# A delta-rule attention and a feed-forward block on one core: the first triangular solve done in two passes by rows

## The chip, the cores and the metric

The kernel runs on one core of a Trainium2 chip. A core has a matrix engine (TensorE, PE in the profile), a vector engine (VectorE, DVE), a scalar engine (ScalarE, ACT), a general engine (GpSimd, POOL) and an engine that here issues the loads and stores (SyncE, SP). Each runs its own list of instructions in order and waits on semaphores. The metric is the device time of one execution in microseconds (us), less being better.

## The reference

The input is q, k, v (4 batches, 8 heads, 768 steps, 48 wide) and beta. A state of 48 by 48 for each batch and head goes through the steps one by one; the answers of all heads are then the tokens (3072 by 384) of a feed-forward block.

```python
k_n = k / (np.linalg.norm(k, axis=-1, keepdims=True) + 1e-06)
for t in range(S):
    kt, vt, bt = (k_n[:, :, t], v[:, :, t], beta[:, :, t, None])
    y[:, :, t] = np.einsum('bhd,bhde->bhe', q[:, :, t], state)
    v_old = np.einsum('bhde,bhd->bhe', state, kt)
    state = state + bt[:, :, :, None] * np.einsum('bhd,bhe->bhde', kt, vt - v_old)
...
x = np.ascontiguousarray(attn_out.transpose(0, 2, 1, 3)).reshape(B * S, H * D)
...
h = x @ w_in          # 384 x 2048
g = h - np.tanh(h)
return (g @ w_out).astype(np.float32)
```

## The kernel before

The 768 steps are cut into 24 chunks of 32. Inside a chunk the recurrence is a linear system: the matrix of inner products of the chunk's keys (the gram, L123), below its diagonal and weighted with beta, plus the identity, has to be inverted for each of the 4 batches and 8 heads. Four chunks make a group (six groups), and one group's 4 x 8 x 4 = 128 systems lie on the 128 partitions of VectorE, which solves them together, column by column: `times` (L246) forms the product of a column with a row, `plus` (L253) adds it to what is left. A group has 30 such columns, and in groups 1 to 5 the middle 21 of them are cut by `spans` into two pieces, so that the second piece of an instruction stands between two that depend on each other.

Group 0 goes another way, since all the rest waits for it. Its four grams are masked and gathered by VectorE (`gather`, L148), turned once (L184), and the 32 x 32 systems are split in halves of 16 (`halves`), which needs 14 columns of 2 x 16 x 16 and then, for each chunk, a join on TensorE of the two halves: `join_a` (L311), a scaled copy on ScalarE (`join_y`, L314), `join_b` (L323), and a last addition on VectorE (`join_u`, L328). Three transposes of half size (L270, L275, L276) lie between.

With the inverse a chunk goes through `chunk` (C, the product with the values, L351), `spread` (sd, L399, a copy on ScalarE or VectorE), `update_product` (U, the state, L361), `answer` (A, L367), `keep` (kp, L402) and the turning of the answer into token columns (`xh`, `xl`). The next chunk begins with `keyed` (K) and `vsub` (vs), which subtracts the state's product, and then its own `chunk`.

Four chunks are a window of 512 tokens of the feed-forward block. There each of 16 blocks of the hidden layer is a product `hidden` (h, L479), `tanh` on ScalarE (th, L487), `gate` on VectorE (ga, L492: h minus tanh h), the split of the result in a high and a low part (gh, L497; gl, L502), and a product `output` (o, L514). Window 0 is done in two halves of 256 columns, so it has 32 gates, the first half with the answers of chunks 0 and 1. All products of the block are in 32-bit parts of that kind, and so the weights too are split on arrival: `sign` (dr, L436) and `low_bits` (db, L442) on ScalarE, `merge` (dm, L447) on VectorE, `high` (dh, L453) on ScalarE, `low` (dl, L457) on VectorE.

The order of every instruction on every engine is written out by hand in one long string, ORDER. An item is engine, operation and arguments: `V:sv:0:40` is step 40 of the solve of group 0 on VectorE, `P:fi:5:-1` is five products of no use (`fill`, L556, 128 x 512 in bf16) on TensorE, `S3:lw:10:1` is the load of weight 10 on SyncE, which may begin when the load three ahead of it has landed (S3: three in flight). The numbers at an item's end are buffers.

## Time and profile before

| | |
|---|---|
| median of three runs | 594.56 us (591.32, 594.56, 595.45) |
| profiled execution: its span | 588.6 us |
| median less the span | 6.0 us (what lies around the span) |
| TensorE busy in the span | 558.4 us, 95% |
| VectorE busy | 379.7 us, 65% |
| ScalarE busy | 187.5 us, 32% |
| GpSimd busy | 39.0 us, 7% |
| read and written in main memory | 42.44 MB and 4.72 MB |

The profile is that of one execution. Its times count from the first instruction, and the 6.0 us are the start and the end around it. Busy shares are means over the whole; the start, up to the first hidden block, and the rest have different limits.

### The profile page before, as it was taken

How to read it: one execution, taken by the hardware profiler on the slowest of the kernel's cores; microseconds unless marked ns; L12 is line 12 of the kernel's file. 1: busy time of each engine (PE TensorE's matmuls, PEld its weight loads, DVE VectorE, ACT ScalarE, POOL GpSimd, SP SyncE). 2: the span in 40 equal slices, each digit the busy share in tenths (PEclk: the TensorE clock that was granted, in tenths of full speed). 3: DMA queues.
4: the chain of work that ended last, by engine and by line, in shares of the span. 5: the costliest groups of instructions: out<-in, count | busy, mean ns of one | idle time of the engine just before them, and what ended most of it. 6: DMA issues, size and time to landing. Idle time of an engine off the chain costs nothing.

```text
span 588.6 us, 25934 instructions
## 1 busy us (share of the span) xinstructions
PE 558.4 (95%) x11943; PEld 458.4 (78%) x11943; DVE 379.7 (65%) x1089; ACT 187.5 (32%) x330; POOL 39.0 (7%) x44
## 2 busy tenths in 40 slices
PE   4848899999999999999999999999999999999997
PEld 3444788899998888788888788787888888888885
DVE  4899997899768995569965333599824322533242
ACT  1447776333313222232222223132320323322211
POOL 0000001100100000000000000200010000001111
PEclk9967999999999999999999999999999999999999
DMA  7778753331325100433312103221210100000001
GB/s 203 236 235 288 220 157 106 107 96 52 105 94 158 47 14 11 144 86 106 91 48 83 30 1 111 70 63 60 62 29 33 52 2 3 1 33 22 2 0 53
DMA packets 21517, 48.82 MB, mean 83 GB/s; under 512 B 3232, under 2 KB 9760, under 8 KB 21408
## 3 DMA queue, kind: packets, MB, share of 16 engines
q1 hardware_dynamic: 20864, 46.44, 26.0%
q8 instruction: 93, 1.52, 1.1%
q10 hardware_dynamic: 544, 0.72, 0.4%
q14 instruction: 16, 0.13, 0.1%
HBM read 42.44 MB, written 4.72 MB: 80 GB/s over the span
## 4 chain that ended last, share of the span: by engine, by line
PE 87%; DVE 9%; issue 2%; DMA 1%; ACT 1%
PE po L514 35%; PE ph L479 34%; PE sums L361 3%; PE g L123 3%; PE pu L351 3%; PE kk L340 3%; PE py L367 2%; PE py L355 2%; DVE ta L246 2%; DVE a L253 2%; PE px L412 1%; DVE raw L447 1%; DMA k<-in_kp 1%; DVE w L457 1%; DMA raw<-in_w_in 1%
## 5 line engine op out<-in xcount | busy, mean ns | idle before, releaser
L514 PE MATMUL po<-gh,w 128*128 128x512 f32 (+1 forms) x1008 | 221.6, 366 | 0.0
L479 PE MATMUL ph<-xt,w 128*128 128x512 f32 (+1 forms) x1008 | 218.4, 364 | 0.5 <-DVE t L492 0.4
L479 PEld LDWEIGHTS ph<-xt,w 128*128 128x128 f32 x1008 | 170.1, 189 | 31.6 <-DVE t L492 0.5
L514 PEld LDWEIGHTS po<-gh,w 128*128 128x128 f32 x1008 | 168.5, 189 | 30.3 <-DVE gh L502 0.2
L492 DVE TENSOR_TENSOR t<-ph,t 128x512 f32<-128x512 f32 (+1 forms) x112 | 68.2, 611 | 108.6 <-ACT t L487 108.4
L487 ACT ACTIVATE t<-ph 128x512 f32<-128x512 f32 (+1 forms) x112 | 59.7, 538 | 192.7 <-PE ph L479 144.7
L502 DVE TENSOR_TENSOR gh<-t,gh 128x512 fp32r<-128x512 f32 (+1 forms) x89 | 54.4, 614 | 26.0 <-ACT gh L497 25.3
L497 ACT CAST gh<-t 128x512 fp32r<-128x512 f32 (+1 forms) x63 | 35.8, 570 | 83.1 <-PE po L514 52.9
L253 DVE TENSOR_TENSOR a<-a,ta 128x108 f32<-128x108 f32 (+28 forms) x269 | 60.4, 257 | 1.5
L246 DVE TENSOR_TENSOR ta<-a 128x108 f32<-128x108 f32 (+28 forms) x269 | 59.6, 254 | 1.3
L502 POOL TENSOR_TENSOR gh<-t,gh 128x512 fp32r<-128x512 f32 (+1 forms) x23 | 27.4, 1193 | 416.9 <-DVE gh L497 215.0
L351 PEld LDWEIGHTS pu<-v,tt 32*32 32x32 f32 x1536 | 27.8, 106 | 9.5 <-issue 4.1
L351 PE MATMUL pu<-v,tt 32*32 32x48 f32 x1536 | 31.6, 212 | 2.4 <-issue 1.4
L340 PEld LDWEIGHTS kk<-st,k 48*32 48x32 f32 x1472 | 27.8, 105 | 6.8 <-issue 3.8
L367 PE MATMUL py<-ub,pc 32*32 32x48 f32 x1536 | 30.9, 209 | 0.4 <-ACT ub L399 0.3
L355 PE MATMUL py<-st,k 48*32 48x48 f32 x1472 | 31.1, 212 | 0.0
L340 PE MATMUL kk<-st,k 48*32 48x48 f32 x1472 | 30.9, 211 | 0.0
L497 DVE CAST gh<-t 128x512 fp32r<-128x512 f32 (+1 forms) x49 | 18.4, 376 | 18.2 <-PE po L514 17.8
L367 PEld LDWEIGHTS py<-ub,pc 32*32 32x32 f32 x1536 | 26.7, 103 | 1.4 <-ACT ub L399 0.6
L355 PEld LDWEIGHTS py<-st,k 48*32 48x32 f32 x1472 | 27.2, 105 | 0.4 <-DVE t L492 0.4
L361 PEld LDWEIGHTS sums<-ub,kt 32*48 32x48 f32 x1472 | 18.9, 119 | 8.4 <-issue 4.7
L361 PE MATMUL sums<-ub,kt 32*48 32x48 f32 x1472 | 21.9, 205 | 1.8 <-ACT ub L399 1.0
(87 smaller groups left out, 386.7 us busy)
## 6 DMA issues: line engine op xcount, KB each, us to landing
c<-in_kp SPq DMA_DIRECT2D x20, 448.0 KB, 4.6
k<-in_kp SPq DMA_DIRECT2D x20, 448.0 KB, 4.0
raw<-in_w_in SPq DMA_DIRECT2D x16, 384.0 KB, 4.1
raw<-in_w_out SPq DMA_DIRECT2D x16, 384.0 KB, 4.2
v<-in_vn SPq DMA_DIRECT2D x24, 192.0 KB, 2.6
kt<-in_kn SPq DMA_DIRECT2D x24, 192.0 KB, 2.9
out<-o SPq DMA_DIRECT2D x17, 256.0 KB, 3.0
k<-in_kp SPq DMA_DIRECT2D x6, 224.0 KB, 4.5
```

Of the source, the lines that this page charges most:

```text
L246: V.tensor_tensor(tv[..., x], P(slice(j + 1, size), slice(j, j + 1)).broadcast_to(d), P(slice(j, j + 1), x).broadcast_to(d), ALU.mult)
L253: V.tensor_tensor(rest, rest, tv[..., x], ALU.add)
L340: nc.tensor.matmul(hv(live[f"kk{s}"])[q:q + 32, h, :], live[f"k{s}"][rows, 0, 2 * h + b // 2, :], states[s % 2][rows, b // 2, h], start=(h ...
L351: nc.tensor.matmul(hv(live[f"pu{s}"])[rows, h, :], tt[rows, 8 * r + h, :], live[f"v{s}"][rows, h, :], start=True, stop=True)
L355: nc.tensor.matmul(hv(live[f"py{s}"])[q:q + 32, h, :], live[f"k{s}"][rows, 1, 2 * h + b // 2, :], states[s % 2][rows, b // 2, h], start=(h ...
L361: nc.tensor.matmul(sums[HALF[b % 2], b // 2, h * D:h * D + D], live[f"kt{s}"][rows, h, :], live[f"ub{s}"][rows, h], start=(s == 0 and h == ...
L367: nc.tensor.matmul(hv(live[f"py{s}"])[to:to + 32, h, :], live[f"pc{s}"][rows, h, :], live[f"ub{s}"][rows, h, :], start=(s == 0 and h == 0) ...
L479: nc.tensor.matmul(p, wi[:, a, c, :], xt[:, b, c, part], start=(i == 0), stop=(i == len(steps_) - 1))
L487: nc.scalar.activation(t, live[name("ph", w, f, z)][:, :n], AF.Tanh)
L492: nc.vector.tensor_tensor(t, live[name("ph", w, f, z)][:, :n], t, ALU.subtract)
L502: (nc.vector if eng == "V" else nc.gpsimd).tensor_tensor(gh[:, 1, :n], live[name("t", w, f, z)][:, :n], gh[:, 0, :n].bitcast(F32), ALU.sub ...
L514: nc.tensor.matmul(live[f"po{NC * w + c}"][:, part], wo[:, a, 128 * c:128 * c + 128], gh[:, b, :n], start=(f == 0 and (a, b) == SPLIT[0] a ...
```

## The change

Group 0 is solved in two passes, chunks 0 and 1 and then 2 and 3 (`rows(0)`, `rows(1)`). Of each pass the two chunks' grams go to one PSUM bank (`grams`), and one transpose reads them from there, without mask or gather, and writes each system twice, into two lanes of 16 partitions for each batch: one lane keeps the even rows of the inverse, the other the odd ones. The inverse starts as the identity (`identity`, on GpSimd) and is built from column 31 down to 1, with `times` (now a scalar_tensor_tensor, whose scalar is read from `gm`, one for each partition) and `plus`, 31 of each in a pass. A transpose of half size (`out_`) hands out each pass's inverse. The joins are gone. The two passes share VectorE: in ORDER their items are interleaved, from step 76 on is the second pass.

Groups 1 to 5 no longer cut their middle columns in two: 60 instructions a group instead of 102, with the same elements. Group 0's beta comes with the constants. All fills use zeros, where they used a block of constants (`wave`) from the second one on. Loads are paced with up to four in flight. The early part of ORDER, up to the first hidden block of window 1 (`P:h:1:0`), is another one; behind it only buffer numbers and the engine of a few items differ (some from GpSimd to VectorE, some from VectorE to ScalarE). In the new order there are 53 fills ahead of chunk 0's `P:C:0`, 11 between it and the first hidden block, and none behind; before there were 29, 31 and 3.

```diff
-    cs = sb.tile([128, 272], F32, name="cs")
+    cs = sb.tile([128, 228], F32, name="cs")
...
-    def gram(s, slot):
-        ps = hc(bank(slot, f"g{s}"))
-        for u in range(16):
-            products(s, ps[:, :, :C], live[f"k{s}"], 0, u)
+    grams = lambda x: sums.rearrange("p r (h c) -> p (r h) c", h=H)[:, :, C * x:C * x + C]
+
+    def gram(s):
+        for r in range(2):
+            for u in range(16):
+                products(s + r, grams(s // 2)[:, H * r:H * r + H], live[f"k{s + r}"], 0, u)
 
     def late(s, slot):
...
     def solve(g, k, *slots):
         if g not in solves:
-            solves[g] = steps(g)
+            solves[g] = steps(g) if g else rows(0) + rows(1)
         solves[g][k](*slots)
 
...
+    def identity():
+        nc.gpsimd.memset(tn, 0.0)
+        for x in range(2):
+            for r in range(2):
+                nc.gpsimd.tensor_copy(tn[:, x].rearrange("p k c -> p (k c)")[:, r::C + 2],
+                                      cs[:, 224 + r:225 + r].broadcast_to([128, C // 2]))
+
+    def rows(x):
+        ss, zz, sq = (small[n] for n in ("ss", "zz", "sq"))
+        nm, gm = small["nm"], half["gn" if x else "gm"]
+        rate, scratch = cs[:, 160 + C * x:160 + C * x + C], (ta, tb)[x]
         V = nc.vector
-        ax = lambda: live[f"a{g}"]
-        sq3 = lambda: ax()[:, :C * C].rearrange("p (i c) -> p i c", c=C)
-        flat = lambda: ax()[:, :C * C]
+        full = lambda: live[f"as{x}"][:, :C * C]
+        a = lambda: full().rearrange("p (i c) -> p i c", c=C)
+        t = tn[:, x]
 
         def turn(slot):
-            make("sol", slot, f"a{g}", [128, 1056])
-            V.transpose(flat(), gs[:, :C * C])
-
-        do = [turn, lambda: V.tensor_copy(sq, flat()[:, ::C + 1])]
-        do.append(lambda: V.tensor_scalar(ss, sq, 1e-30, None, ALU.max))
-        if g == 0:
...
                 lambda: V.tensor_scalar(nm, nm, 0.5, None, ALU.mult)]
         else:
-            do.append(lambda: V.tensor_scalar(nm.bitcast(I32), ss.bitcast(I32), -0.5, 1597463007.0, ALU.mult, ALU.add))
-            for _ in range(3):
-                do += [
-                    lambda: V.scalar_tensor_tensor(zz, ss, -0.5, nm, ALU.mult, ALU.mult),
-                    lambda: V.tensor_tensor(zz, zz, nm, ALU.mult),
-                    lambda: V.scalar_tensor_tensor(nm, zz, 1.5, nm, ALU.add, ALU.mult)]
+            do += newton(nm, ss, zz, sq, gm) + [lambda: V.scalar_tensor_tensor(gm, gm, -1.0, rate, ALU.mult, ALU.mult)]
+        do.append(lambda: V.transpose(turned[x], nm))
+
+        def times(j):
+            k, n = j // 2, C // 2 - j // 2
+            to = scratch[:, j % 2 * 136:j % 2 * 136 + n * j].rearrange("p (k c) -> p k c", c=j)
+            V.scalar_tensor_tensor(to, t[:, k:, j:j + 1].broadcast_to([128, n, j]), gm[:, j:j + 1],
+                                   a()[:, j:j + 1, :j].broadcast_to([128, n, j]), ALU.mult, ALU.mult)
+
+        def plus(j):
+            k, n = j // 2, C // 2 - j // 2
+            V.tensor_tensor(t[:, k:, :j], t[:, k:, :j], scratch[:, j % 2 * 136:j % 2 * 136 + n * j].rearrange("p (k c) -> p k c", c=j), ALU.add)
+
+        for j in range(C - 1, 0, -1):
+            do += [lambda j=j: times(j), lambda j=j: plus(j)]
+        do.append(lambda: V.scalar_tensor_tensor(t, t, -1.0, gm[:, None, :].broadcast_to([128, C // 2, C]), ALU.mult, ALU.mult))
+
+        def out_(slot=None):
+            if x == 0:
+                make("sol", slot, "tt0", [128, 1024])
+            to = live["tt0"][:, :32 * C].rearrange("p (u k z) -> p k z u", k=C // 2, z=2)[:, :, :, 16 * x:16 * x + 16]
+            V.transpose(to, t.rearrange("p k (z u) -> p k z u", z=2))
+
+        do.append(out_)
+        return do
...
-        def spans(j):
-            if nb == 2 or not 5 < j < 27:
-                return (slice(0, j),)
-            x = 4 if j < 14 else 10
-            return (slice(0, x), slice(x, j))
+            n = C - 1 - j
+            return ta[:, j % 2 * 240:j % 2 * 240 + n * j].rearrange("p (i c) -> p i c", c=j), [128, n, j]
 
         def times(j):
             tv, dims = scratch(j)
-            for x in spans(j):
-                d = dims[:-1] + [x.stop - x.start]
-                V.tensor_tensor(tv[..., x], P(slice(j + 1, size), slice(j, j + 1)).broadcast_to(d),
-                                P(slice(j, j + 1), x).broadcast_to(d), ALU.mult)
+            V.tensor_tensor(tv, sq3()[:, j + 1:, j:j + 1].broadcast_to(dims), sq3()[:, j:j + 1, :j].broadcast_to(dims), ALU.mult)
 
         def plus(j):
             tv, _ = scratch(j)
-            for x in spans(j):
-                rest = P(slice(j + 1, size), x)
-                V.tensor_tensor(rest, rest, tv[..., x], ALU.add)
-
-        for j in range(1, size - 1):
...
-    def join_u(s):
-        gs, tn, tt, x = parts(s)
-        upper = tt[:, x:x + 8, C // 2:]
-        nc.vector.scalar_tensor_tensor(upper, jh(live[f"jb{s}"]), half_, upper, ALU.mult, ALU.add)
-
...
     def prep(s, eng):
         g, r = divmod(s, 4)
         v = live[f"v{s}"]
+        nt = live[f"nt{g}"] if g else turned[r // 2]
         (nc.vector if eng == "V" else nc.gpsimd).tensor_tensor(
-            v, v, live[f"nt{g}"][:, 8 * r:8 * r + 8, None].broadcast_to([128, H, D]), ALU.mult)
+            v, v, nt[:, 8 * (r if g else r % 2):, None][:, :8].broadcast_to([128, H, D]), ALU.mult)
 
     def key_product(s, h, b):
...
-                fill_ = wave if fills[0] else wz
-                fills[0] += 1
-                nc.tensor.matmul(ps.rearrange("p (a b) -> p a b", a=4), fill_, wide(fill_, 4), start=True, stop=True)
+                nc.tensor.matmul(ps.rearrange("p (a b) -> p a b", a=4), wz, wide(wz, 4), start=True, stop=True)
...
-V:open A:ka:3:0 S3:lk:2:1 S3:lk:0:2 A:const A:ka:1:3 P:gm:3:0 P:gm:2:1 S2:lb:0:0 P:gm:0:2 S2:lc:4:0 V:gr:0:V:0
...
+V:open A:ka:0:0 A:const G:ti S1:lk:1:1 P:fi:5:-1 P:fi:5:-1 S2:lw:4:0 S3:lk:2:2 S3:lk:3:3 S4:lw:2:1 S4:lq:2:0 S4:lc:5:0
```

On VectorE, in the middle of the first solve, the list before was this (`a` is the matrix being solved, `ta` scratch; L447 and L457 are weights):

```order
L253 TENSOR_TENSOR a_229<-a_229,ta 128x2x4x11
L246 TENSOR_TENSOR ta<-a_229 128x72
L457 TENSOR_TENSOR w_433<-raw_231,w_433 128x2x384
L253 TENSOR_TENSOR a_229<-a_229,ta 128x2x3x12
L246 TENSOR_TENSOR ta<-a_229 128x52
L253 TENSOR_TENSOR a_229<-a_229,ta 128x2x2x13
L246 TENSOR_TENSOR ta<-a_229 128x28
L253 TENSOR_TENSOR a_229<-a_229,ta 128x2x14
```

and now it is this (`ta`, `tb` scratch of the first and second pass, `tn` the inverse being built, `as` the turned grams):

```order
L215 SCALAR_TENSOR_TENSOR ta<-tn,gmh,as_324 128x126
L215 SCALAR_TENSOR_TENSOR tb<-tn,gnh,as_342 128x56
L220 TENSOR_TENSOR tn<-tn,ta 128x9x14
L220 TENSOR_TENSOR tn<-tn,tb 128x2x28
L215 SCALAR_TENSOR_TENSOR ta<-tn,gmh,as_324 128x130
L215 SCALAR_TENSOR_TENSOR tb<-tn,gnh,as_342 128x81
L220 TENSOR_TENSOR tn<-tn,ta 128x10x13
L220 TENSOR_TENSOR tn<-tn,tb 128x3x27
```

Where each step stood next to the one that it depends on, or to a piece of the weights, the steps of the two passes now stand in turn, and the second pass lags behind.

On ScalarE, ahead of the spread of chunk 0 (the copy `ub` of L399, now L365), the list before was this (`pc` and `yj` are copies out of PSUM, `w` and `raw` weights):

```order
L314 ACTIVATE yj_913<-ja_812 128x128
L453 CAST w_954<-raw_523 128x2x384
L314 ACTIVATE yj_961<-ja_674 128x128
L436 ACTIVATE raw_541<-raw_541 128x768
L453 CAST w_968<-raw_427 128x2x384
L442 ACTIVATE raw_541<-raw_541,cs 128x768
L399 COPY ub_981<-pu_915 128x384
L436 ACTIVATE raw_851<-raw_851 128x768
```

and now it is this (`ta` of 128x1 is the load of the tanh table):

```order
L155 COPY pc_600<-l_499 128x256
L408 ACTIVATE raw_108<-raw_108,cs 128x768
L295 ACT_TABLE_LOAD
L295 ACTIVATE ta<-ta 128x1
L402 ACTIVATE raw_401<-raw_401 128x768
L419 CAST w_672<-raw_122 128x2x384
L408 ACTIVATE raw_401<-raw_401,cs 128x768
L365 COPY ub_840<-pu_785 128x384
```

The spread stands behind one load of the table and fewer copies of weights, and the copies for the joins are gone; what is directly ahead of it is `low_bits` of weights 0 and 1, as before.

## Rows read from the trace of the kernel before

**Rows 1.** The span in 40 slices, busy tenths of TensorE and VectorE.

```profile
PE   4848899999999999999999999999999999999997
...
DVE  4899997899768995569965333599824322533242
```

**Rows 2.** Long windows: busy us (instructions) by engine, clock, DMA share, GB/s.

```profile
11.10:47.10 36.00, 22.85 (x925) 15.36 (x926) 31.89 (x103) 15.81 (x26) 3.01 (x7) 0.83 0.79 242
47.10:66.30 19.20, 16.63 (x548) 10.06 (x549) 19.20 (x63) 15.50 (x24) 0.00 (x0) 0.87 0.87 270
66.30:168.40 102.10, 98.76 (x2865) 93.08 (x2863) 89.85 (x279) 46.44 (x90) 7.35 (x8) 1.00 0.38 112
66.30:178.20 111.90, 108.29 (x3288) 101.53 (x3286) 94.38 (x289) 48.31 (x93) 8.08 (x9) 1.00 0.36 107
178.20:588.60 410.40, 406.54 (x6928) 327.79 (x6928) 231.39 (x632) 106.36 (x187) 27.66 (x24) 1.00 0.17 51
```

**Rows 3.** Timeline of VectorE at the start of the solve: start us, us.

```profile
7.82 1.47 DVE L148 TENSOR_TENSOR gs<-g,cs 128x256 f32<-128x256 f32 x3 [5.97 <-PE g L123]
...
11.17 1.25 DVE L184 STREAM_TRANSPOSE a<-gs 128x1024 f32<-128x1024 f32 x1
```

**Rows 4.** Timeline of TensorE: grams, chunk 0, first hidden blocks of windows 0 and 1.

```profile
5.07 2.72 PE L123 MATMUL g<-k 48*32 48x32 f32 x192 [5.07 <-DMA k<-in_kp]
...
47.10 1.49 PE L351 MATMUL pu<-v,tt 32*32 32x48 f32 x61 [0.49 <-ACT pc L155]
...
66.36 2.51 PE L479 MATMUL ph<-xt,w 128*128 128x256 f32 x18
...
178.10 6.56 PE L479 MATMUL ph<-xt,w 128*128 128x512 f32 x27
```

**Rows 5.** Timeline of VectorE: the 32nd gate, the last of window 0.

```profile
168.35 0.42 DVE L492 TENSOR_TENSOR t<-ph,t 128x256 f32<-128x256 f32 x1 [0.41 <-ACT t L487]
```

**Rows 6.** Timeline of VectorE: solve steps, a dependent pair and two neighbours.

```profile
21.95 0.28 DVE L246 TENSOR_TENSOR ta<-a 128x112 f32<-128x112 f32 x1
22.26 0.28 DVE L253 TENSOR_TENSOR a<-a,ta 128x112 f32<-128x112 f32 x1
...
44.91 0.40 DVE L246 TENSOR_TENSOR ta<-a 128x96 f32<-128x96 f32 x2
45.23 0.55 DVE L335 TENSOR_TENSOR v<-v,nt 128x384 f32<-128x384 f32 x1
```

**Rows 7.** VectorE groups by shape, whole span: busy us, mean ns of one.

```profile
L447 DVE SCALAR_TENSOR_TENSOR raw<-raw 128x768 int32<-128x768 int32 x16 | 15.2, 952 | 0.0
...
L502 DVE TENSOR_TENSOR gh<-t,gh 128x256 fp32r<-128x256 f32 x27 | 11.9, 441 | 0.9 <-ACT gh L497 0.6
...
L280 DVE STREAM_TRANSPOSE tt<-a 128x1024 f32<-128x1024 f32 x5 | 10.4, 2074 | 0.0
...
L184 DVE STREAM_TRANSPOSE a<-gs 128x1024 f32<-128x1024 f32 x6 | 7.4, 1232 | 0.2
...
L497 DVE CAST gh<-t 128x256 fp32r<-128x256 f32 x17 | 4.9, 285 | 2.2 <-PE po L514 2.1
...
L246 DVE TENSOR_TENSOR ta<-a 128x170 f32<-128x170 f32 x5 | 1.7, 333 | 0.1
...
L328 DVE SCALAR_TENSOR_TENSOR tt<-jb,cs,tt 128x128 f32<-128x128 f32 x4 | 1.4, 346 | 0.0
```

**Rows 8.** Timeline of ScalarE: the spread of chunk 0.

```profile
52.62 0.47 ACT L399 COPY ub<-pu 128x384 f32<-128x384 f32 x1
```

**Rows 9.** Window of the loads up to the weights that chunk 0 meets.

```profile
0.00:46.00 46.00, 26.29 (x1153) 18.54 (x1157) 33.62 (x102) 16.87 (x26) 3.21 (x11) 0.88 0.77 227
```

**Rows 10.** Windows of 2 us around the clock's fall and rise.

```profile
44.00:46.00 2.00, 1.43 (x38) 0.61 (x42) 1.97 (x11) 0.57 (x1) 0.00 (x0) 0.50 0.85 280
...
52.00:54.00 2.00, 1.05 (x65) 0.81 (x64) 2.00 (x5) 1.93 (x3) 0.00 (x0) 1.00 0.90 287
```

**Rows 11.** Timeline of TensorE: the fills before the rise.

```profile
49.10 3.09 PE L556 MATMUL po<-cs 128*128 128x512 bf16 x7
```

More of the change, by code (lines that the diff above doesn't have):

```diff
@@ L798 @@
     bt = by_parity(beta.reshape(B, H, NS, C).transpose(2, 0, 1, 3).copy())
[L799 to L800 removed]
+    lanes = lambda a: a.reshape(-1, 4, B, H, C).transpose(0, 2, 1, 3, 4).reshape(-1, 128, C)
+    first = lanes(bt[[0, 1, 0, 1, 2, 3, 2, 3]])
+    bt = lanes(bt)
+    const = np.zeros((128, 228), np.float32)
     p, i = np.arange(128)[:, None], np.arange(C)
```

496 lines of the change are left out of this document (229 added, 267 removed).

## The prediction

> **What bounds the kernel now.** The busy shares of the page mislead here: TensorE is at 95% and VectorE at 65% over the whole span, but the slices show two stages [rows 1]. In the first four or five slices VectorE is at 8 or 9 tenths and TensorE often below; after that TensorE stands at 9 to the end and VectorE falls. So I cut the span at the events that matter and read the windows [rows 2]. From the turn of the first solve (11.17, [rows 3]) to chunk 0 (47.10, [rows 4]) VectorE is busy 31.89 of 36.00 us, and from there to the first hidden block (66.36, [rows 4]) all of 19.20. The start is VectorE's. From 66.3 to the last gate of window 0 (168.35, [rows 5]) both are nearly full: TensorE 98.76 of 102.10, VectorE 89.85. From the first hidden block of window 1 (178.10, [rows 4]) on it is TensorE alone, 406.54 of 410.40 [rows 2], and there the change leaves the work as it was. So the question is at what time window 1 begins; what is saved or lost before 178.10 goes one for one into the end.
>
> The account of VectorE to that point: 168.35 - 11.17 = 157.2 us, in which it is idle 4.1, 0 and 12.25 us (the three windows of [rows 2]), so 16.4 idle and 140.8 busy. Window 1 begins 9.75 us behind the 32nd gate [rows 4, 5].
>
> **The work that VectorE gets.** What one step costs must be read from start to start, because an instruction's end overlaps the next one's start. A dependent step of 112 elements starts 0.31 us ahead of the next [rows 6]. The slope from 170 elements (333 ns) to 768 (952 ns) is 619/598 = 1.04 ns an element [rows 7]; the dependent step's fixed part is then 0.31 - 0.116 = 0.19 us. Two neighbours that don't wait for each other, of 168 elements together, take 0.32 us [rows 6], so 0.07 each and the slope. I take 0.07 as the price of a step that has another lane's step behind it.
>
> - Elements of the solves. Group 0 had 28 instructions with 2,240 elements; now it has 4 x 31 = 124 (31 `times` and 31 `plus` in each of two passes) with 4 x 2,856 = 11,424, the sum of (16 - j/2 rounded down) times j over j from 1 to 31. Of groups 1 and 2, whose solves lie ahead of the 32nd gate, 204 instructions become 120, with the same 19,840 elements. So 9,184 elements more: 9,184 x 1.04 = +9.6 us.
> - Their fixed part. The count goes from 232 to 244: +0.8 us if all hide. In group 0's new order 115 of the 124 steps have a neighbour that doesn't need them, as the order of VectorE shows; in groups 1 and 2 each of 120 steps now waits for the one before unless something stands between, and there the order puts gates, weights and gathers between most. I take +1.0, with the upper bound that every one of 115 pays 0.12 more (0.19 - 0.07), +13.8, as a rival of its own below.
> - The scalar from a pointer in 62 `times`. The nearest row is the old join, the same operation with a pointer, 128 elements in 346 ns [rows 7], against 0.29 by slope for 128 elements without one (333 - 42 x 1.04). That is 0.05 at most, since it also reads PSUM; at least 0. I take 0.03: +1.9 (0 to 3.1).
> - Transposes. Away go one of 1.23 [rows 7] and three of half size at some 1.04 (half of 2.07, [rows 7]): 4.35. In come two turns and two of half size. A turn of 1,024 elements reads PSUM with a stride; a contiguous one takes 1.23, one with a strided output 2.07 [rows 7]. I take 1.85, nearer the second, as every element hops: 3.7 + 2.1 = 5.8, so +1.4 (0.1 to 1.9). The Trainium skill, "Vector Engine (DVE) Microarchitecture Reference", section 5.2, "Measured stream behaviour on trn2", has 1.73 ns a column for one source that hops at each element, against 1.054; that is for SBUF and for no transpose, and it would make a turn 1.8 us, an estimate; no run here has shown it yet.
> - Work that changes hands. To VectorE come four `low` parts of a gate at some 0.34 and three scalings of values at some 0.47 (their rows, 441 ns [rows 7] and 0.55 [rows 6], less the overlap of about 0.1): +2.8. From it go five casts (285 ns, [rows 7]), two gathers, and four copies to ScalarE, estimated together at -4.2; the joins' four additions, at about 0.2 each, and a scaling, -1.0.
>
> Sum: 9.6 + 1.0 + 1.9 + 1.4 + 2.8 - 4.2 - 1.0 = **+11.5**, so 152.3 us busy where 140.8 were. With the bounds above, about +8 to +14.
>
> **What VectorE no longer waits for.** The masked gathers begin at 7.82, the turn at 11.17 [rows 3]. The three grams that start when the keys land take 2.72 us from 5.07 [rows 4], 0.9 each. The new turn needs two: 5.07 + 1.8 = 6.9, and I say 7.0. That is 4.2 us of start. With no wait at all the 32nd gate would stand at 7.0 + 152.3 = 159.3. Before, the waits were 16.4 in the same stretch, 4.1 early and 12.25 while TensorE was almost full. They don't all go, since TensorE's own work stands between: gates need hidden blocks, `vsub` needs the state.
>
> Early waits, from the new order of VectorE and ScalarE: merging of weight 4 behind its load, the first turn of group 1 behind the pair of grams that stands behind 14 fills, a merge and a `low` behind ScalarE's chain, POOL's triangle; an estimate of 4.5 us together, like the 4.1 before. Chunk 0: its spread on ScalarE started at 52.62 [rows 8], behind splits of weights. In the new order the splits of weights 0 and 1 are still ahead of it. By the order 10.5 MB are loaded up to weight 1, which at 227 GB/s [rows 9] is 46 us, and with the splits behind it 48 to 49; so the spread comes some 3.5 us earlier, and the first hidden block with it at about 63.5 (61.5 to 66.4). Four in flight rather than three I cost at nothing: the share of the DMA engines is already 0.77 to 0.87 there [rows 2, 9].
>
> From there TensorE has, by [rows 2], 108.29 us of work to 178.10, less three small products and fills that now stand ahead or are gone, an estimate of 3.5: 104.8. If it idled as little as before (3.3 of 102.10, [rows 2]) window 1 would begin at 63.5 + 104.8 + 3.3 = 171.6, seven earlier than before. But VectorE cannot follow: its 32nd gate, with the 4.5 early and some 4.6 of waits later, stands at 159.3 + 9.1 = 168.4, window 1 at 168.4 + 9.75 = 178.15. That is the time of before. The late waits of 4.6 are the weakest number; 12.25 was seen with less work to do. When VectorE is the later of the two its waits shrink, and I take a little over a third.
>
> So span 588.6 + 0.05, and the time is **594.6** by the profiled execution (588.6 + 6.0); the median of the runs shown is 594.56, the same. I write 595.
>
> **Rivals.**
>
> *VectorE keeps up.* Its added work is at the lower bounds (+8) and the late waits fall to 1: 7.0 + 148.8 + 5.5 = 161.3, window 1 by VectorE at 171.1 and by TensorE at 171.6. Seven earlier: 588. For it: 12.25 us of idle time stand in VectorE's window. Against: they came where TensorE was at 97%, so each waits for something that won't come sooner unless the start does. 586 to 589.
>
> *The clock.* The granted clock was 0.50 in the window from 44 to 46 and 1.00 from 52 on [rows 10]; between stand seven fills [rows 11] and what follows. Half of full speed is the lower of its two levels, 1.2 of 2.4 GHz. In the new order 11 fills stand between chunk 0 and the first hidden block where 31 stood, and they are zeros throughout. If the clock is still at half when the hidden blocks begin, a stretch of 10 to 20 us of products at half speed loses 5 to 10, on the engine that has no slack afterwards: 600 to 605. It decides from the granted clock of the 2 us stretches from the first hidden block: at 0.5 this holds, at 1.0 it doesn't. For it: where the clock was at half TensorE was busy 1.43 of 2 us [rows 10], and the stretch from chunk 0 on has 20 fills less now. Against: 53 fills ahead of chunk 0, and the first hidden blocks are dense themselves.
>
> *The lanes don't hide each other.* If a step of one pass costs the dependent price although the other's stands between, the start gets +13.8 us, of which the early waits take back about 4: window 1 at 188, 604. For it: a lane's steps are written as chains. Against: the neighbours of [rows 6] took 0.16 us each for 84 elements on the mean, where a dependent step of that size would take 0.19 + 0.09 = 0.28. The Trainium skill says in "VectorE: DVE Perf Modes", section "The DRAIN you can't avoid", that the next operation does not start until the pipe is empty, and advises fewer operations; by that rule alone this rival holds, and the two neighbours of this trace, started 0.16 us apart, speak against it.
>
> *It doesn't do what it says:* the weights' loads hold chunk 0 where it was (first hidden block at 66). VectorE is then late anyway, and it costs 0 to 2 us: inside the forecast.
>
> **How the numbers follow.** A measurement of this kernel can tell about 1% from no change, 5.9 us: faster is below 588.6, slower above 600.5. The forecast, 591 to 599, has 0.58; VectorE keeping up 0.20 (half to two thirds of it below 588.6, and some of it below 586); the clock 0.13; the lanes 0.09. To leave out no more than 2 in 10 the range goes from 585 to 604. Faster 0.18: most of the first rival and the forecast's lower tail. Slower 0.22: the two others. Same 0.60.
>
> **What would show it.** In the profile after: the first turn at 7.0 and of 1.85 us; steps of L215 and L220 that start 0.07 us plus 1.04 ns an element apart; the spread of chunk 0 at 49, the first hidden block at 63.5, the 32nd gate at 168.4, window 1 at 178.2; VectorE idle 9 us up to that gate, and TensorE idle some 7 from 63.5 on, waiting for gates. I would be wrong if VectorE were idle as before in the stretch with the gates: then its work was never what set that pace, and the earlier start is a gain, or if the granted clock is 0.5 past 62.

## The result and the profile after

The changed kernel took 596.86 us (median of 20 runs, 594.74 to 601.77) where the kernel before took 593.95 (20 runs, 589.45 to 598.03): 1.0063 of its time, 95% interval 1.0039 to 1.0087. It was measured again beside the experiments, on two chips: 1.0136 (1.0091 to 1.0181) and 1.0116 (1.0088 to 1.0144). So it is slower by 0.6 to 1.4%. All ratios, and the medians of e0 and e11 below, leave out the one execution in each of those two runs that was in a slower state of the chip. The time of 595 and the range hold; what the sum rested on does not in every part.

First the slices, which show the same two stages as [rows 1]: VectorE (DVE) at 9 tenths from the second slice to the eleventh, TensorE (PE) at 9 from about the sixth. The third line is the clock granted to TensorE.

```profile
PE   4676699999989999999999999999999999999997
...
DVE  2999999999967997468984444498925322533142
...
PEclk8576989999989999999999999999999999999999
```

The long windows, cut at the same events as [rows 2] (first turn, chunk 0, first hidden block, 32nd gate, first hidden block of window 1):

```profile
11.10:46.90 35.80, 21.00 (x559) 11.56 (x559) 34.86 (x145) 12.98 (x19) 1.31 (x1) 0.67 0.79 245
46.90:68.00 21.10, 15.16 (x657) 10.50 (x657) 19.70 (x66) 13.74 (x21) 0.16 (x1) 0.76 0.63 197
68.00:173.00 105.00, 98.71 (x2618) 93.06 (x2607) 97.18 (x255) 53.61 (x105) 1.42 (x2) 0.97 0.36 109
68.00:183.70 115.70, 107.84 (x3039) 101.34 (x3027) 102.06 (x265) 55.45 (x108) 1.42 (x2) 0.97 0.35 106
183.70:594.50 410.80, 407.32 (x6930) 327.82 (x6928) 232.44 (x509) 106.55 (x187) 23.81 (x21) 1.00 0.17 51
```

VectorE is idle 0.9, 1.4 and 7.8 us in the first three, 10.1 in all, where it was 16.4; from 183.7 on TensorE is alone, 410.8 us to the end as against 410.4 in [rows 2]. Everything that the change did is over by then.

The start. TensorE's grams of the four chunks, and then VectorE's first turn, with some steps of the two passes behind it:

```profile
5.04 1.29 PE L123 MATMUL sums<-k 48*32 48x32 f32 x128
7.28 0.76 PE L123 MATMUL sums<-k 48*32 48x32 f32 x64 [0.95 <-DMA k<-in_kp]
8.20 0.38 PE L123 MATMUL sums<-k 48*32 48x32 f32 x21 [0.17 <-DMA k<-in_kp]
10.52 0.58 PE L123 MATMUL sums<-k 48*32 48x32 f32 x43 [1.94 <-issue]
```

```profile
11.14 1.25 DVE L194 STREAM_TRANSPOSE as<-sums 128x1024 f32<-128x1024 f32 x1 [10.13 <-PE sums L123]
...
30.16 0.34 DVE L215 SCALAR_TENSOR_TENSOR ta<-tn,gmh,as 128x130 f32<-128x130 f32 x1
30.43 0.29 DVE L215 SCALAR_TENSOR_TENSOR tb<-tn,gnh,as 128x81 f32<-128x81 f32 x1
30.64 0.28 DVE L220 TENSOR_TENSOR tn<-tn,ta 128x130 f32<-128x130 f32 x1
30.84 0.23 DVE L220 TENSOR_TENSOR tn<-tn,tb 128x81 f32<-128x81 f32 x1
31.00 0.34 DVE L215 SCALAR_TENSOR_TENSOR ta<-tn,gmh,as 128x120 f32<-128x120 f32 x1
```

The two grams that the first turn needs are done at 5.04 + 1.29 = 6.33. The turn starts at 11.14, when the last 43 products of the gram of chunk 3 have ended (10.52 + 0.58 = 11.10). That is where [rows 3] had it, not at 7.0. (The grams of both passes lie in one PSUM tile, `sums`, of two banks: chunks 0 and 2 in one bank, 1 and 3 in the other, and not each pass in a bank of its own.) The steps run as lanes: from 30.16 to 31.00 four of them, 130, 81, 130 and 81 elements, take 0.84 us.

From chunk 0 to the first hidden block, TensorE, with the spread of chunk 0 on ScalarE:

```profile
46.88 0.88 PE L317 MATMUL pu<-v,tt 32*32 32x48 f32 x64 [1.50 <-DVE zz L241]
...
53.10 0.76 PE L333 MATMUL py<-ub,pc 32*32 32x48 f32 x25 [2.61 <-issue]
...
64.59 1.07 PE L123 MATMUL g<-c 48*32 48x64 f32 x84
66.57 0.69 PE L123 MATMUL g<-c 48*32 48x64 f32 x44 [0.90 <-issue]
67.19 0.93 PE L327 MATMUL sums<-ub,kt 32*48 32x48 f32 x64
68.05 1.33 PE L445 MATMUL ph<-xt,w 128*128 128x256 f32 x9
```

```profile
47.82 0.48 ACT L365 COPY ub<-pu 128x384 f32<-128x384 f32 x1 [2.83 <-PE pu L317]
...
64.77 0.49 ACT L386 CAST xt<-px 128x384 fp32r<-128x384 f32 x1
```

Chunk 0 stands at 46.88 as before (47.10, [rows 4]); its spread comes 4.8 us earlier than in [rows 8], since less is queued ahead of it. But the first hidden block comes at 68.05, 1.7 later than in [rows 4]. Between them TensorE stopped twice for no wait on another engine that the timeline shows ("issue": 2.61 us ahead of 53.10, 0.90 ahead of 66.57), and the pair of grams of chunks 8 and 9 and the update of chunk 1, which stood behind the first hidden blocks, now stand ahead of them (64.59 to 68.05). The last copy of the high part of the answers (`xt`) had ended at 65.26, 2.8 us before the block.

The 32nd gate and window 1:

```profile
172.97 0.41 DVE L458 TENSOR_TENSOR t<-ph,t 128x256 f32<-128x256 f32 x1
```

```profile
183.67 1.67 PE L445 MATMUL ph<-xt,w 128*128 128x512 f32 x6
```

They are 4.6 and 5.6 us later than in [rows 5] and [rows 4], and that is, but for 0.3 us, the 5.9 by which the span grew (594.5 against 588.6).

Part of this is TensorE's. First TensorE in the changed kernel, then in the kernel before, from the last update ahead of the 32nd gate; then VectorE in the changed kernel, and a window of it (the third number from the end is the granted clock):

```profile
168.37 0.47 PE L327 MATMUL sums<-ub,kt 32*48 32x48 f32 x10 [2.26 <-issue]
168.77 2.29 PE L480 MATMUL po<-gh,w 128*128 128x256 f32 x9
170.86 1.62 PE L445 MATMUL ph<-xt,w 128*128 128x256 f32 x9
```

```profile
165.65 0.93 PE L361 MATMUL sums<-ub,kt 32*48 32x48 f32 x64
166.51 1.33 PE L479 MATMUL ph<-xt,w 128*128 128x256 f32 x9
167.68 1.24 PE L514 MATMUL po<-gh,w 128*128 128x256 f32 x9
```

```profile
171.10 0.29 DVE L463 CAST gh<-t 128x256 fp32r<-128x256 f32 x1 [3.14 <-PE po L480]
```

```profile
168.30:171.80 3.50, 3.43 (x24) 3.34 (x24) 0.67 (x3) 0.00 (x0) 0.00 (x0) 0.51 0.76 221
```

TensorE stops for 2.26 us in the middle of the update of chunk 7, and from 168.3 to 171.7 its clock is at the lower level, so that the nine products of `po` take 2.29 us where they take 1.24 in the kernel before. VectorE, done at 167.95 with what stands ahead in its list, waits 3.14 us for them. All eleven traces of the new order (the experiments' among them) have a stop of 1.70 to 2.26 us at this place and behind it a wait of VectorE of 1.5 to 3.1 us, and all but e3's have the fall of the clock by it; the three traces of the old order (before, e4, e11) have no stop there and no single wait of VectorE over 0.61. No run took the stop away.

The times of one execution are to be compared with care here. In the result every execution's time stands beside its span: 596.47 and 594.5 for the one above, so that 2.0 us lie around a span, not 6.0. For the kernel before, beside the experiments, it is 1.7 to 1.8. The trace of before, 588.6, was therefore an execution of some 590.3 us, one of the faster ones of its kernel (589.45 to 598.03), and the two traces differ by 5.9 us where the medians differ by 2.9.

### The profile page after: what moved, and what is told of

Same layout as the page of the kernel before. It is cut to its first block, busy times and chain, and to the rows that moved or that the text cites. A ratio compares the mean times of both kernels' runs of the same rounds, so it can differ in the third digit from the quotient of the medians.

```text
span 594.5 us, 24796 instructions
## 1 busy us (share of the span) xinstructions
PE 558.3 (94%) x11432; PEld 455.1 (77%) x11432; DVE 389.2 (65%) x984; ACT 190.2 (32%) x337; POOL 28.5 (5%) x34
## 3 DMA queue, kind: packets, MB, share of 16 engines
q8 instruction: 89, 1.46, 1.0%
## 4 chain that ended last, share of the span: by engine, by line
PE 81%; DMA 10%; DVE 6%; issue 1%; ACT 1%; SPq 0%; ACTq 0%
PE po L480 34%; PE ph L445 32%; DMA c<-in_kp 4%; PE sums L327 3%; DMA raw<-in_w_out 3%; PE pu L317 3%; PE kk L306 2%; PE py L333 2%; PE py L321 2%; PE g L123 2%; DMA raw<-in_w_in 2%; DMA k<-in_kp 1%; PE px L378 1%; DVE w L423 1%; DVE a L277 1%
## 5 line engine op out<-in xcount | busy, mean ns | idle before, releaser
L480 PE MATMUL po<-gh,w 128*128 128x512 f32 (+1 forms) x1008 | 224.4, 369 | 0.0
L453 ACT ACTIVATE t<-ph 128x512 f32<-128x512 f32 (+1 forms) x112 | 59.6, 537 | 183.7 <-PE ph L445 146.8
L468 DVE TENSOR_TENSOR gh<-t,gh 128x512 fp32r<-128x512 f32 (+1 forms) x97 | 57.7, 599 | 31.2 <-ACT gh L463 30.5
L463 ACT CAST gh<-t 128x512 fp32r<-128x512 f32 (+1 forms) x68 | 37.8, 558 | 92.4 <-PE po L480 54.0
L277 DVE TENSOR_TENSOR a<-a,ta 128x30 f32<-128x30 f32 (+9 forms) x150 | 49.9, 333 | 2.9
L273 DVE TENSOR_TENSOR ta<-a 128x30 f32<-128x30 f32 (+9 forms) x150 | 49.1, 327 | 3.0
L468 POOL TENSOR_TENSOR gh<-t,gh 128x512 fp32r<-128x512 f32 x15 | 19.3, 1290 | 277.7 <-ACT gh L463 162.7
L463 DVE CAST gh<-t 128x512 fp32r<-128x512 f32 (+1 forms) x44 | 17.0, 387 | 21.1 <-PE po L480 20.6
L123 PE MATMUL g<-c 48*32 48x64 f32 x1280 | 17.1, 242 | 11.5 <-DMA c<-in_kp 6.9
```

Of the source, the lines that this page charges most:

```text
L273: V.tensor_tensor(tv, sq3()[:, j + 1:, j:j + 1].broadcast_to(dims), sq3()[:, j:j + 1, :j].broadcast_to(dims), ALU.mult)
L277: V.tensor_tensor(sq3()[:, j + 1:, :j], sq3()[:, j + 1:, :j], tv, ALU.add)
L453: nc.scalar.activation(t, live[name("ph", w, f, z)][:, :n], AF.Tanh)
L463: (nc.scalar.copy if eng == "A" else nc.vector.tensor_copy)(gh[:, 0, :n], live[name("t", w, f, z)][:, :n])
L468: (nc.vector if eng == "V" else nc.gpsimd).tensor_tensor(gh[:, 1, :n], live[name("t", w, f, z)][:, :n], gh[:, 0, :n].bitcast(F32), ALU.sub ...
L480: nc.tensor.matmul(live[f"po{NC * w + c}"][:, part], wo[:, a, 128 * c:128 * c + 128], gh[:, b, :n], start=(f == 0 and (a, b) == SPLIT[0] a ...
```

## The experiments

The theory is that of the prediction, called V: up to window 1 the time is VectorE's list, its first turn plus its work plus what it waits. The rival, T: TensorE's own work and its granted clock set that time, and VectorE only waits more or less. This table holds what the timelines and windows of all runs say (us; busy and idle are VectorE's from the first turn to the 32nd gate, so that first turn, busy and idle add up to the gate in every row; what tests V is how they move against each other):

| kernel | first turn | chunk 0 | first hidden | 32nd gate | window 1 | busy | idle | span |
|---|---|---|---|---|---|---|---|---|
| before | 11.17 | 47.10 | 66.36 | 168.35 | 178.10 | 140.85 | 16.3 | 588.6 |
| after | 11.14 | 46.88 | 68.05 | 172.97 | 183.67 | 151.71 | 10.1 | 594.5 |
| after again (e0) | 11.92 | 47.64 | 69.55 | 172.16 | 182.53 | 151.73 | 8.5 | 593.5 |
| after again (e12) | 11.39 | 47.15 | 69.29 | 174.72 | 184.96 | 152.03 | 11.3 | 596.1 |
| earlier turn (e1) | 6.29 | 42.03 | 63.04 | 166.84 | 178.28 | 151.86 | 8.7 | 589.7 |
| columns in pieces (e2) | 11.37 | 47.11 | 69.87 | 175.19 | 185.62 | 155.04 | 8.8 | 596.5 |
| fills not zero (e3) | 11.37 | 47.11 | 69.02 | 171.15 | 184.03 | 151.91 | 7.9 | 594.9 |
| work back to GpSimd (e5) | 11.37 | 47.14 | 67.55 | 171.93 | 182.43 | 151.62 | 8.9 | 593.2 |
| 4 sums more, early (e6) | 10.85 | 51.25 | 72.11 | 177.15 | 189.28 | 156.38 | 9.9 | 600.9 |
| 4 sums more, late (e7) | 11.43 | 47.18 | 69.93 | 179.63 | 189.79 | 156.09 | 12.1 | 600.8 |
| steps left out (e8) | 7.24 | 39.66 | 63.82 | 166.24 | 176.56 | 142.60 | 16.4 | 588.3 |
| before, earlier keys (e11) | 10.64 | 47.96 | 66.81 | 168.28 | 178.25 | 138.79 | 18.8 | 588.3 |
| casts to ScalarE (e9) | 7.12 | 42.95 | 66.22 | 169.26 | 180.14 | 150.01 | 12.1 | 591.6 |
| before, whole columns (e4) | 11.19 | 48.74 | 68.16 | 172.59 | 184.74 | 139.16 | 22.2 | 594.7 |

In all of them 410 to 412 us lie between window 1 and the end of the span. A trace is of one execution, which need not stand near the median of its kernel: e4's is the slowest of twelve (596.45 us, median 589.79), e1's the fastest of six (591.64, median 595.92).

**The changed kernel again (e0, e12), as a mark.**

> The changed kernel once more, as the mark for the others of this chip: 1.006 of the time before, 596 to 597 us. In its trace VectorE's work from the first turn to the 32nd gate should be 151 to 152 us again; no theory expects anything else.

> The changed kernel as the mark for this chip: 1.006 to 1.014 of the time before.

Measured: 598.91 us against 590.40 of before on the same chip, and 597.29 against 590.19 on another; the ratios are those above. VectorE's work is the same to 0.3 us in the three traces, while its first turn moves by 0.8 us and its idle time by 2.8. A gain of under 2 us is not to be read from one trace.

**The first turn without the grams of chunks 2 and 3 ahead of it (e1).** A part of one line of ORDER:

```diff
-P:gm:0 P:gm:2 P:sp:4:0:1 V:sv:0:0:0
+P:gm:0 V:sv:0:0:0 P:gm:2 P:sp:4:0:1
```

> The grams of chunks 2 and 3 are issued behind the first turn and not ahead of it. Theory V (VectorE's list sets the start of window 1): the first turn begins at 6.4 to 7 us instead of 11.1, of these 4.5 us some are lost to loads that VectorE then meets earlier, and the end moves by 2.5 to 4.5: 592 to 594 us. Rival T (TensorE's own work and its granted clock set it): VectorE only waits longer, the end moves by less than 1 us: 596 to 597.

Measured: 595.92 us, 1.0103 of before (1.0066 to 1.0140), on the chip on which the changed kernel took 598.91 (1.0136). VectorE's first turn, and TensorE's grams of chunks 2 and 3 behind it:

```profile
6.29 1.25 DVE L194 STREAM_TRANSPOSE as<-sums 128x1024 f32<-128x1024 f32 x1 [5.28 <-PE sums L123]
```

```profile
7.59 1.01 PE L123 MATMUL sums<-k 48*32 48x32 f32 x85 [1.35 <-DVE as L194]
```

The turn starts as soon as its own two grams are there; the other two wait for it now (7.59). From there all events of the table come 4 to 6.5 us earlier than in e0, with the same work and the same idle time, and window 1 at 178.28. Between the two executions traced that is 3.8 us (591.64 against 595.48): V's shift, and not T's. The time does not settle it. The two intervals of the ratios overlap, 595.92 lies above V's 592 to 594, and e9 below, which is faster than the changed kernel, holds another edit besides. What speaks for a real shift is that window 1 begins at 176.56 to 180.14 in the three traces with this edit (e1, e8, e9) and at 182.43 to 185.62 in the six of the new order without it and without added work.

**Columns in pieces again (e2), and the kernel before with whole columns (e4).**

```diff
+        def spans(j):
+            if not 5 < j < 27:
+                return (slice(0, j),)
+            x = 4 if j < 14 else 10
+            return (slice(0, x), slice(x, j))
...
+            for x in spans(j):
+                V.tensor_tensor(sq3()[:, j + 1:, x], sq3()[:, j + 1:, x], tv[..., x], ALU.add)
```

> Groups 1 to 5 have their 21 middle columns in two pieces again, as before the change; all else is the changed kernel. Between the two traces the steps of groups 1 and 2 went from 37.5 us in pieces to 35.1 us whole. Theory V: VectorE gets 2.4 us more ahead of the 32nd gate, the time goes up by 1 to 2.4 us: 598 to 599.5. Rival (the pieces hide the wait of a step for the one before, and taking them away was what cost): 2 to 4 us less: 593 to 595. Rival T: no change.

Measured: 598.99 us, 1.0144 (1.0118 to 1.0170) beside e0's 1.0136. VectorE's work rises by 3.3 us (155.04 against 151.73), somewhat more than expected; in the time 1 to 2 us more can't be told from none, since e0 itself is known to 0.45%. Of the rival's 2 to 4 us less the two intervals leave some 2.6 at the most; e4 tries it where the noise is smaller.

```diff
-            if nb == 2 or not 5 < j < 27:
-                return (slice(0, j),)
-            x = 4 if j < 14 else 10
-            return (slice(0, x), slice(x, j))
+            return (slice(0, j),)
```

> The kernel before with one edit: the columns of groups 1 to 5 are no longer cut in two. Theory V: VectorE has 2.4 us less to do ahead of the 32nd gate, but TensorE was at 97% there; 0 to 2 us less than before (ratio 0.997 to 1.000). Rival (the pieces hide waits, so that whole columns cost): 2 to 4 us more (1.003 to 1.007).

Measured: 589.79 us against 591.25, 0.9983 (0.9948 to 1.0017). Within V's bounds, not distinct from no change, and outside the rival's 1.003. Whole columns were no part of the loss. Its one trace shows how much an execution can lose with no more work on VectorE: window 1 at 184.74 with 139.16 us of work and 22.2 us idle, while TensorE stopped for 1.26 us ahead of 98.69 and 2.23 ahead of 176.38 and its clock was at the lower level from 99.7 to 103.1.

**Fills that are not zero (e3).**

```diff
+        nc.scalar.dma_start(wzf, const[:, 228:292])
...
-P:fi:5:-1 P:fi:5:-1 S2:lw:4:0
+P:fi:5:-1 P:fi:5:-1 A:wv S2:lw:4:0
```

> The fills behind the first ten use the block of cosines of the kernel before, loaded by one small transfer of its own, instead of zeros. Theory V: no change, 596 to 597 us. Rival T in the form of the clock: the granted clock is at full from about 26 us on and not at half in the stretches around 33, 50 to 58 and 77, TensorE gains 2 to 5 us: 592 to 595.

Measured: 598.75 us, 1.0142 (1.0106 to 1.0177), beside e0's 1.0136: no gain. Windows of the changed kernel in the result, then of the changed kernel again (e0), then of this run; the third number from the end is the granted clock, 0.50 being the lower of its two levels (1.2 of 2.4 GHz):

```profile
68.00:70.00 2.00, 1.38 (x21) 1.12 (x9) 2.00 (x6) 1.53 (x3) 0.00 (x0) 1.00 0.94 309
```

```profile
68.00:70.00 2.00, 2.00 (x75) 1.82 (x67) 1.92 (x6) 1.84 (x4) 0.00 (x0) 0.50 0.86 332
```

```profile
68.00:70.00 2.00, 2.00 (x60) 1.91 (x53) 2.00 (x7) 2.00 (x4) 0.00 (x0) 0.50 0.83 320
```

Here the clock is at the lower level from 68 to 70, where the trace in the result has it at full; but e0's, with zeros in its fills, has it at the lower level there too. So this run did not make another clock than the changed kernel has by itself, and it says nothing on the data of the fills, and little on the price of the clock. What the three traces do show is that the place of the low clock up to 80 us does not decide window 1 (183.67, 182.53 and 184.03). The most that it cost VectorE up to there is the 1.4 us of the trace in the result, where VectorE waited for TensorE between chunk 0 and the first hidden block.

**Work back to GpSimd (e5).** Three scalings of values and five `low` parts of window 0, in ORDER:

```diff
-V:pr:1:V ... V:gl:0:5:0:V ... V:gl:0:13:1:V
+G:pr:1:G ... G:gl:0:5:0:G ... G:gl:0:13:1:G
```

> Eight pieces of work of window 0 (three scalings of values, five low parts of a gate) go back from VectorE to GpSimd, where they were before; 3.1 us of VectorE by the prices in the prediction. Theory V: 1.5 to 3 us less than the changed kernel: 593.5 to 595. Rival T: no change, 596 to 597. A third: GpSimd's slower copy (1.2 us against 0.44) makes a block of TensorE wait and it costs 1 to 2 us.

Measured: 597.09 us, 1.0105 (1.0078 to 1.0132), within the changed kernel's own 1.006 to 1.014; V's 593.5 to 595 was missed. The changed kernel did not run on this chip, so the time does not tell 1.5 to 3 us from nothing. The trace tells why there may be little: the work left VectorE's list (30 `low` parts ahead of the 32nd gate became 26, 9 scalings 6), yet its busy time stayed, 151.62 against 151.73. VectorE's `low` parts (busy us, mean ns of one) in e0 and then in e5, and an instruction of GpSimd in e5 with the one of VectorE that ran beside it:

```profile
L468 DVE TENSOR_TENSOR gh<-t,gh 128x256 fp32r<-128x256 f32 x30 | 12.3, 418 | 1.3 <-ACT gh L463 1.2
```

```profile
L468 DVE TENSOR_TENSOR gh<-t,gh 128x256 fp32r<-128x256 f32 x26 | 11.8, 459 | 1.3 <-ACT gh L463 1.2
```

```profile
109.88 1.29 POOL L292 TENSOR_SCALAR_AFFINE_SELECT a<-a 128x1024 f32<-128x1024 f32 x1
```

```profile
109.97 1.46 DVE L468 TENSOR_TENSOR gh<-t,gh 128x256 fp32r<-128x256 f32 x1
```

Instructions that were not touched became longer, but only those that ran beside one of GpSimd's, which was busy 8.69 us in place of 2.89. Against the median of their own shape, the 18 of VectorE's instructions that overlapped with GpSimd's took 3.0 us more, and the other 433 none; in e0 it is 0.8 us more in 8. So 2.2 us came back of the 2.8 at which I had priced this term.

**VectorE's work made longer (e6, e7).** A sum of no use, 1,024 elements, four times:

```diff
+    def extra():
+        nc.vector.tensor_reduce(ex, cs[:, None, 0:128].broadcast_to([128, 8, 128]), mybir.AxisListType.X, ALU.add)
```

> Four sums of no use on VectorE (1,024 elements each, some 1.1 us, 4.4 together) between steps 20 and 46 of the first pass, ahead of chunk 0. Theory V: 3 to 4.5 us more than the changed kernel: 599.5 to 601. Rival T: under 1 us more.

> The same four sums, 4.4 us of VectorE, between gates 3 and 14 of window 0. Theory V: 3 to 4.5 us more than the changed kernel: 599.5 to 601. If VectorE sets the time only up to the first hidden block and TensorE from there on: under 1.5 us more.

Measured: 603.51 us, 1.0211 (1.0192 to 1.0230), with the sums early; 602.91, 1.0214 (1.0190 to 1.0238), with the sums late. Against the 1.0105 of e5 on the same chip that is 1.1%, 6.3 us, for 4.8 us of sums (1.21 us each), and against the changed kernel's marks (1.0063 to 1.0136) 4.4 to 9 us. The windows from the first turn to the 32nd gate (behind the length come the busy times of TensorE, of its loads, and of VectorE):

```profile
10.85:177.15 166.30, 134.59 (x3818) 115.69 (x3819) 156.38 (x466) 80.91 (x145) 2.90 (x4) 0.88 0.49 147
```

```profile
11.43:179.63 168.20, 138.74 (x3818) 117.22 (x3819) 156.09 (x466) 80.33 (x145) 2.89 (x4) 0.86 0.47 145
```

VectorE is busy 156.4 and 156.1 us, 4.4 to 4.7 more, and idle no less than before. So VectorE's added work comes out at the end, within these bounds whole, also when it stands between the gates, where TensorE was at 97% before the change. T as the only cause falls, and so does the thought that VectorE counts only up to the first hidden block. That TensorE's stop ahead of the 32nd gate costs time too is not touched by this: both traces have it.

**VectorE's work made shorter (e8).** Columns 9 to 22 of both passes are left out, so that part of group 0's inverse is missing, with e1's order. A part of one changed line of ORDER:

```diff
-V:sv:0:94 V:sv:0:56 V:sv:0:109 V:sv:0:57 V:sv:0:110 V:sv:0:58
+V:sv:0:94 V:sv:0:109 V:sv:0:110 V:sv:0:58
```

> The kernel with the earlier first turn, and of both passes of the first solve the columns 9 to 22 are left out (56 of 124 steps, 6,916 elements), so that part of the inverse is not computed: about 11 us less of VectorE's work, about what it had before the change, with the early start. Theory V (VectorE's work sets the start of window 1 until TensorE is full): 8 to 11 us less than the earlier turn alone until TensorE stops it; window 1 at about 171, 0.5 to 1.5% faster than before (585 to 588 us on a chip where before takes 591). Rival T: as with the earlier turn alone, 1% slower than before.

Measured: 591.68 us, 1.0008 (0.9979 to 1.0036). 56 steps less (9.3 us of busy time) and the time is that of the kernel before, not 0.5 to 1.5% below it. The window from the first turn to the 32nd gate has idle time back, 159.00 - 142.60 = 16.4 us:

```profile
7.24:166.24 159.00, 133.19 (x3944) 115.77 (x3945) 142.60 (x407) 79.79 (x145) 2.85 (x4) 0.89 0.52 160
```

Where it went is on ScalarE, in the timeline, and in TensorE's waits:

```profile
40.66 0.90 ACT L402 ACTIVATE raw<-raw 128x768 f32<-128x768 f32 x1 [6.79 <-DMA raw<-in_w_in]
...
43.11 0.45 ACT L365 COPY ub<-pu 128x384 f32<-128x384 f32 x1
...
62.42 0.60 ACT L150 COPY gs<-g 128x256 f32<-128x256 f32 x1 [4.70 <-PE g L123]
```

```profile
PE g L123 <- DMA c<-in_kp: 3.1, 1, 3.1
```

Chunk 0's product is ready at 39.66 + 0.88, but its spread comes at 43.11: ScalarE waited 6.79 us for the load of weight 0 or 1 that is queued ahead of it. At 62.42 its copies of the grams of chunks 8 and 9 come after 4.70 us, because these grams waited 3.1 us for their keys. So V's size is right upward and stops soon downward: of 9.3 us taken off, 1.7 are seen in window 1 (176.56 against e1's 178.28, which is of e1's fastest execution) and 5.6 between the two ratios (on two chips). A few microseconds behind VectorE stand the loads, in the order in which they are issued.

**The earlier turn, and twelve casts from VectorE to ScalarE (e9).** One of the twelve casts; e1's edit stands beside them:

```diff
-V:gh:0:3:0:V:1
+A:gh:0:3:0:A:1
```

> The kernel with the earlier first turn, and the twelve casts of window 0's gates that VectorE still did (0.29 us each, 3.4 in all, ten of them ahead of the 32nd gate) go to ScalarE. Theory V: 2 to 3 us less than the earlier turn alone (ratio to before 1.005 to 1.007). If ScalarE's copy comes later than VectorE's did: no gain, 1.010.

Measured: 592.25 us, 1.0038 (1.0016 to 1.0061), where the changed kernel on the same chip took 597.29 (1.0116, 1.0088 to 1.0144). The intervals are apart: 0.8%, 4.6 us. VectorE's work falls by 1.9 us against e1, and its idle time rises by 3.4; in VectorE's waits (total, times, longest) it now waits 6.5 us for those casts, where it waited 1.6 in e1:

```profile
DVE gh L468 <- ACT gh L463: 6.5, 6, 1.9
```

The trace has window 1 at 180.14, later than e1's, which is of a faster execution; how much of the gain is the casts and how much the turn is not settled by this.

**The kernel before, with whole columns and earlier keys of chunk 1 (e11).** Besides e4's edit:

```diff
-V:open A:ka:3:0 S3:lk:2:1 S3:lk:0:2 A:const A:ka:1:3
+V:open A:ka:3:0 A:ka:1:3 S3:lk:2:1 S3:lk:0:2 A:const
```

> The kernel before, with whole columns in groups 1 to 5 and with the keys of chunk 1 issued ahead of the constants, so that the fourth gather (10.55 us) and the first turn (11.17) come earlier. Theory V: the turn 0.5 to 1.5 us earlier, the end by as much and up to 1 us for the whole columns: ratio 0.996 to 0.998. Rival: the constants come later and the masks wait for them: 1.000.

Measured: 590.05 us, 1.0007 (0.9975 to 1.0039): the turn came at 10.64 in place of 11.17, VectorE had 2.1 us less to do, and the time did not change. That is the rival's 1.000, though not for its reason, and not V's 0.996 to 0.998: VectorE's idle time grew by 2.5 us instead. In the kernel before, VectorE's list is not what sets window 1. No version here is faster than the kernel before.

## Why the prediction was right, and where it was not

The forecast was that a saving at the start is eaten by more work on VectorE, with the end where it was. The end is 0.6 to 1.4% later. Its main step, that added work of VectorE is paid at the end, held; that the figure came so near is luck, since errors stood against each other in three places. By its steps:

- **What bounds the kernel** held. From window 1 on nothing moved (410 to 412 us in all traces), and added work on VectorE ahead of it came out at the end (e6, e7).
- **The work that VectorE gets** held as a sum, 152.3 forecast and 151.71 measured, by terms that offset each other. Added up from start to start in the timeline, the 62 `times` take 15.34 us and the 62 `plus` 10.72, 26.1 where group 0's 28 steps took 7.8; the 120 whole steps of groups 1 and 2 take 35.1, some 2.4 less than the pieces. Together +15.9 (15.7 without the short gaps between steps), where I had 9.6 + 1.0 + 1.9 = 12.5. A `plus` costs (10.72 - 5,712 x 0.00104) / 62 = 0.077 us besides its elements, as forecast. A `times` costs 0.15, not 0.10: it costs 0.06 to 0.075 more than a `plus`, above the end of the range that I had for its pointer (no run tells the pointer from the other operation), and the higher figure holds one that ran 1.27 us for 70 elements, while GpSimd's triangle was at work:

```profile
39.29 1.27 DVE L215 SCALAR_TENSOR_TENSOR ta<-tn,gmh,as 128x70 f32<-128x70 f32 x1
```

```profile
39.19 1.31 POOL L292 TENSOR_SCALAR_AFFINE_SELECT a<-a 128x1024 f32<-128x1024 f32 x1 [31.78 <-DVE sq L260]
```

 Against that a turn from PSUM took 1.25 us and not 1.85; the row that it equals is the contiguous one [rows 7], not the one with a strided output to which I put it nearest. The Trainium skill's 1.73 ns a column ("Vector Engine (DVE) Microarchitecture Reference", section 5.2, "Measured stream behaviour on trn2") is for SBUF and did not carry over: 1,024 elements in 1.25 us are 1.22 ns each. All transposes together cost 0.15 us more than before, where I had +1.4. The rest, each instruction counted up to the start of the next: scalings and `low` parts +1.9 (forecast 2.8), casts, gathers and copies -4.8 (forecast -4.2), joins and small steps -1.9 (forecast -1.0). So the solve was 3.2 too cheap in the sum and all else 3.8 too dear.
- **What VectorE no longer waits for** failed at its first number, "the new turn needs two". It waited for four grams: both passes' grams lie in one PSUM tile, the other two stood ahead of the turn in ORDER, and it started 0.04 us behind the last of them. e1 shows it, since with these two behind the turn it starts at 6.29, where the prediction had 7.0; its window 1 at 178.28, where the prediction had 178.15, is of its fastest execution and no more than near. The idle time was forecast at 9.1 and measured 10.1 (8.5 to 11.3 in the three traces), but its parts were not: 2.3 us up to the first hidden block where I had 4.5, and 7.8 behind it where I had 4.6. Of these 7.8, 3.1 are the wait behind TensorE's stop, for which the prediction has no term. TensorE's own idle time, forecast at some 7 for waiting on gates, is 7.9 from the first hidden block to window 1, and 4.3 of that are its stops.
- **The first hidden block** was forecast 3.5 us earlier with the spread of chunk 0. The spread came earlier (47.82, forecast 49), the block did not. I had taken the three small products that moved ahead of it off TensorE's later work, and had not put them on the way to the block; they, and the stop of 0.90 us among them, are 2.8 of the 4.5 us by which it missed 63.5 (65.26 to 68.05). The late first turn and the stop of 2.61 us are the rest; how it is shared between them is not shown.
- **How the trace stands to the median** failed too. I took 6.0 us to lie around the span; for the kernel before it is 1.7 to 1.8. So an execution of before that was quicker than its median was set equal to the median, which put the forecast 4.3 us above that execution's own time, and this went against the 5.5 us by which window 1 came late. The forecast of 595 is as near to 596.86 as it is because these two errors stood against each other, and that is luck.
- **The rivals.** VectorE keeping up: no; even with 9.3 us of its work left out it did not come below the kernel before, since the loads stood next (e8). The clock: the price of 5 to 10 us did not come, but the sign that I gave for being wrong, 0.5 past 62, did. It was 1.00 from 62 to 70 in the trace of the result and 0.50 there in e0's, with window 1 at 183.67 and 182.53, so in that stretch it decides nothing. From 168.3 to 171.7 it was at half with TensorE busy throughout and VectorE waiting; there the 18 products of `po` and `ph` took 1.3 us more than in the kernel before (2.29 and 1.62 against 1.24 and 1.33). From the first hidden block to window 1 the mean was 0.95 to 0.98 in the eleven traces of the new order, 0.98 to 1.00 in the three of the old order. The lanes: they hide each other, by the 0.077 of a `plus`. The rule of the Trainium skill ("VectorE: DVE Perf Modes", section "The DRAIN you can't avoid") that the next operation starts when the pipe is empty does not describe these rows, where the step of 81 elements started 0.27 us behind a step of 130 that lasts 0.34; they agree with what the same section adds, "A next op that is not held starts earlier".

So the account of the trace is this: 10.9 us more work on VectorE up to the 32nd gate, 6.2 us less waiting, and a start that came no earlier, which gives the 4.6 us by which the gate is late; 1 us more follows up to window 1, where TensorE stopped for 0.92 us ahead of 179.16. That the work is paid is shown by adding to it and by leaving some of it out. How much of the loss is TensorE's stop ahead of the gate is open: without the 3.1 us for which VectorE waited behind it the gate would be some 1.5 us late, an estimate from this trace.

## What to carry to other kernels

A first step that reads a shared tile waits for all that is issued into that tile ahead of it; put into the order only what it needs, and look up in the trace what ended its wait. Work moved to an engine that is already the pace costs its full price at the end, while work taken off it is worth something only up to the next limit, here the loads, a few microseconds behind; adding work and leaving work out shows both. A chain of engine times that adds up is no cause yet: look at what each wait ended on, here once a stop of the engine that was thought to be ahead. Before a trace is set against a median, find out which time belongs to that trace's own execution.
